# Re-timing the loads of the weights and of pair 2, one copy moved to VectorE and one changed order of masks, in a fused state-space and feed-forward kernel

## The chip, the cores and the metric

The kernel runs on one core of a Trainium2 chip. The metric is the device time in microseconds (us). Five runs of the kernel before gave 131.43, 131.52, 131.6, 133.93 and 136.94 us, with a median of 131.6 us. One execution was profiled.

TensorE appears in the profile as PE (matrix multiplications) and PEld (its weight loads), VectorE as DVE, ScalarE as ACT, GpSimd as POOL and the sync engine as SP. A small q behind a name means the engine's instruction sequencer, which also issues DMAs.

## The reference

The first half is a state-space layer over `x` (4 batches, 8 heads, 768 rows, 32 columns), with a decay `a` for each row and with `B` and `C` of 16 columns for each head. The second half is a bilinear feed-forward layer: 3072 tokens of 256 columns, a hidden width of 1536.

```python
for c in range(nc):                                  # chunks of 32 rows
    cum = np.cumsum(la, axis=-1)                     # la = log(a) of the chunk
    L = np.exp(cum[..., :, None] - cum[..., None, :]) * causal
    CB = np.einsum('bhin,bhjn->bhij', Cc, Bc)
    y_intra = np.einsum('bhij,bhjd->bhid', CB * L, xc)
    y_inter = np.einsum('bhin,bhnd->bhid', Cc, state) * np.exp(cum)[..., None]
    y[:, :, sl] = y_intra + y_inter
    state = decay_full * state + sum_j(B_j x_j decay_from_j)
...
x = y.transpose(0, 2, 1, 3).reshape(B * S, H * D)
out = ((x @ w_a) * (x @ w_b)) @ w_out
```

Inputs and output are float32.

## The kernel before

**Tiling.** The kernel works in 6 blocks of 128 rows and not in chunks of 32. A "pair" is one block of two batches, so there are 12 pairs, numbered 0 to 11: pairs 0 and 1 are block 0, pairs 2 and 3 are block 1, and so on. A tile of a pair holds 64 partitions for each of its two batches (`bt` 0 and 1); every partition holds two neighbouring rows.

**A pair's way through the engines.**

1. Loads (`load1`, line 119): six DMAs for a pair, B, C and x, one for each batch. B and C are 64 KB each and x is 128 KB each in the profile's counting. B and C arrive in pieces of 128 bytes, x in pieces of 256 bytes. The input tiles `bn`, `cn` and `xn` have three buffers each.
2. Scaling: `scale_bc` (line 236) makes `cm` and `bm` in f16 from C and B and the decay factors `fC` and `fB`; `scale_x` (line 227) makes `x16`. From pair 1 on, GpSimd scales B and C.
3. `transposes` (line 253): TensorE transposes `bm` (two instructions) and `cm` (two) into PSUM. ScalarE copies the transposed B out twice (`bt`, line 265), then the transposed C is copied out (`ct`, line 266). For pair 0 the transposes go to two PSUM banks and VectorE copies C. For all other pairs they go to one bank, `TT`, which is a part of the tile `SC0`, and ScalarE copies C.
4. `scores` (line 271): 32 small matmuls into the four banks `SC[0]` to `SC[3]`. Two tiles hold them: `SC0` has banks 0 and 1, `SC1` has banks 2 and 3.
5. `mask` (line 304): four products with the causal mask, 128x512 each, on VectorE. In pairs 0 to 2 one of the four goes another way (`by_pool`): ScalarE copies the scores to `tmp`, and GpSimd multiplies.
6. `pv` (line 348): matmuls with the carried state (`sbd`, line 355), with `x16` (line 321) and for the next state (line 338), all into `SC1`; ScalarE copies the result into `X2T`.
7. `state` (line 381): VectorE updates `U32`; GpSimd spreads it into `sbd` for the pair two further on.
8. `unit(p, k2)` (line 410), six for each pair: eight matmuls make 256 of the 1536 hidden columns for Wa and Wb, ScalarE copies the one half (`asb`), and the product with the other half is a VectorE instruction. `unit` returns this product as a function, so that the caller chooses where in VectorE's queue it goes: `h = unit(...)` and later `h()`. `go` calls both at once.
9. `out_half` (line 456): twelve matmuls with Wo, a copy on ScalarE and a store from SP's queue.

**What sets the order.** The order is written out by hand, and each engine executes its own instructions in this order. Semaphores stand between engines where one reads what another wrote. Two instructions of different engines that touch the same PSUM tile are kept apart too, also where both only read. PSUM holds `SC0`, `SC1` and four more banks, taken in turn by the tag `ff`.

**The start.** The weights are split in thirds of 512 hidden columns. The units 0 and 1 of a pair use the first third of Wa and Wb, units 2 and 3 the second, units 4 and 5 the third. GpSimd's queue issues the weights (`load_w`, line 169), with a conversion to f16 in the DMA. Two dependencies are written by hand: the second Wa waits for one of pair 0's x loads (line 182), and pair 3's first load waits for Wo (line 504). SP's queue issues most of the input loads, ScalarE's queue a few of pair 0 and 1. Matmuls on a tile of zeros (`warmup`, line 184) fill TensorE's first microseconds.

Of the kernel before, what the change touches and what calls it, by code (L numbers as in the profile page):

```python
# [15 lines left out]
AFTER = mybir.DependencyInfo(mybir.DependencyClass.Sync, mybir.DependencyReason.DATA)  # L16
# [6 lines left out]
def kernel(  # L23
# [13 lines left out]
    nc = tc.nc  # L37
# [4 lines left out]
    NBLK = S // Q  # L42
# [36 lines left out]
    Wa = big.tile([128, 2, d_ff], f16, name="Wa")  # L79
    Wb = big.tile([128, 2, d_ff], f16, name="Wb")  # L80
    Wo = big.tile([128, NK, d_model], f16, name="Wo")
# [9 lines left out]
    fC = big.tile([128, NBLK, 2, NBP, H], f32, name="fC")  # L91
# [21 lines left out]
    def tiles(p):  # L113
        Bn = inp.tile([128, H, 2, N], f32, name="bn", tag="bn")
        Cn = inp.tile([128, H, 2, N], f32, name="cn", tag="cn")
        Xn = inp.tile([128, H, 2, D], f32, name="xn", tag="xn")
        pair_in[p] = (Bn, Cn, Xn)

    def load1(eng, p, which, bt):
        blk, bp = divmod(p, NBP)  # L120
        src = (B, C, x)[which][2 * bp + bt, :, blk * Q : (blk + 1) * Q, :]
        return eng.dma_start(  # L122
            pair_in[p][which][64 * bt : 64 * bt + 64].rearrange("i h r n -> i h (r n)"),
            src.rearrange("h (i r) n -> i h (r n)", r=2),
        )

    def load(p, eng=None):
        tiles(p)
        return [load1(eng or nc.sync, p, w, bt) for w in range(3) for bt in range(2)]
# [6 lines left out]
    load1(nc.scalar, 0, 1, 1)  # L136
    load1(nc.sync, 0, 1, 0)
    nc.scalar.preload_act_table_set("natural_log_exp_and_others")
    x_in = load1(nc.scalar, 0, 2, 1)
    nc.scalar.dma_start(c32, p32_t.ap())  # L140
    load1(nc.sync, 0, 2, 0)
    load1(nc.scalar, 1, 1, 1)
# [2 lines left out]
    load1(nc.sync, 1, 0, 1)  # L145
    load1(nc.sync, 1, 2, 0)
    load1(nc.sync, 1, 2, 1)
    load(2)
    nc.vector.memset(warm.bitcast(u32), 0)  # L149
    nc.vector.memset(zero, 0.0)  # L150
    nc.gpsimd.memset(sel, 1.0)
# [14 lines left out]
    KC = 4 * 128  # L166
    wd = []

    def load_w(q3):
        for W, src in ((Wa, moe_w_a), (Wb, moe_w_b)):  # L170
            c = slice(q3 * KC, (q3 + 1) * KC)
            wd.append(nc.gpsimd.dma_start(W[:, :, c], src.rearrange("(f p) e -> p f e", p=128)[:, :, c]))

    load_w(0)
    nc.gpsimd.memset(causal, 1.0)
    for bt in range(2):
        v = causal[64 * bt : 64 * bt + 64]
        nc.gpsimd.affine_select(
            out=v, in_=v, compare_op=ALU.is_ge, fill=0.0, base=0, pattern=[[-1, 2], [1, Q]], channel_multiplier=-2
        )  # L180
    load_w(1)
    tc.add_manual_dep(wd[2].ins, x_in.ins.name, AFTER, reason="inputs first")

    def warmup(n, bank, cols=512):
        for _ in range(n):
# [5 lines left out]
    def scan(lo, hi):  # L191
        for k in range(lo, hi):
            nc.vector.tensor_tensor_scan(Pr[:, k], a_sb[:, k], zero, 1.0, ALU.mult, ALU.add)
# [27 lines left out]
    def flat(f, lo, hi):  # L221
        return f[:, lo:hi].rearrange("p k r b h -> p (k r b h)")
# [4 lines left out]
    def scale_x(p, eng):  # L227
        X16 = mid.tile([128, H, 2, D], f16, name="x16", tag="x16")
        xo, xi = X16.rearrange("p h r d -> p (h r d)"), pair_in[p][2].rearrange("p h r d -> p (h r d)")
        st.setdefault(p, {})["X16"] = X16  # L230
        if eng is nc.scalar:
            nc.scalar.mul(xo, xi, XS)  # L232
        else:
            eng.tensor_scalar(xo, xi, XS, None, ALU.mult)  # L234

    def scale_bc(p, which, eng):
        blk, bp = divmod(p, NBP)
        name, f = (("bm", fB), ("cm", fC))[which]
        m_ = mid.tile([128, 2, H, N], f16, name=name, tag=name)
        eng.tensor_tensor(  # L240
            out=m_,
            in0=pair_in[p][which].rearrange("p h r n -> p r h n"),
            in1=f[:, blk, :, bp].unsqueeze(3).broadcast_to((128, 2, H, N)),
            op=ALU.mult,
        )
        st.setdefault(p, {})[name] = m_

    def scale(p):
        scale_bc(p, 1, nc.gpsimd)
        scale_bc(p, 0, nc.gpsimd)  # L250
        scale_x(p, nc.gpsimd)

    def transposes(p, ps=None):
        s = st[p]
        TB, TC = (TT[:, 0:256], TT[:, 256:512]) if ps is None else [t_.bitcast(f16)[:, 0:256] for t_ in ps]
        for T_, src in ((TB, s["bm"]), (TC, s["cm"])):
            for r in range(2):
                nc.tensor.transpose(  # L258
                    T_[:, r * 128 : (r + 1) * 128], src[:, r].rearrange("p h n -> p (h n)"), ident
                )  # L260
        BT = mid.tile([128, 2, 2, 2, 64], f16, name="bt", tag="bt")
        CT = mid.tile([128, 2, Q], f16, name="ct", tag="ct")
        for e in range(2):
            o_ = BT[:, e].rearrange("p r t i -> p (r t i)")
            nc.scalar.activation(out=o_, in_=TB, func=AF.Copy, scale=par[:, e : e + 1])  # L265
        (nc.scalar.copy if ps is None else nc.vector.tensor_copy)(  # L266
            CT.rearrange("p t (i r) -> p r (t i)", r=2), TC.rearrange("p (r c) -> p r c", r=2)
        )
        s["BT"], s["CT"] = BT, CT
# [20 lines left out]
    def product(p, m):  # L290

        return (
            st[p]["T1"][:, 2 * m : 2 * m + 2].rearrange("p e r q -> p e (r q)"),
            SC[m].rearrange("p (e c) -> p e c", e=2),
        )

    def product0(m2, e):

        return (
            st[0]["T1"][:, 4 * m2 : 4 * m2 + 4].rearrange("p (m e) r q -> p e m (r q)", e=2)[:, e],  # L300
            (SC0, SC1)[m2][:, :, e * 256 : e * 256 + 256],
        )

    def mask(out_in, by_pool=False):
        o_, i_ = out_in
        c_ = causal.rearrange("p r q -> p (r q)").unsqueeze(1).broadcast_to((128, 2, 2 * Q))
        if by_pool:
            tmp = mid.tile([128, 2, 2 * Q], f32, name="tmp", tag="tmp")
            nc.scalar.copy(tmp, i_)  # L309
            nc.gpsimd.tensor_tensor(out=o_, in0=tmp, in1=c_, op=ALU.mult)  # L310
        else:
            nc.vector.tensor_tensor(out=o_, in0=i_, in1=c_, op=ALU.mult)  # L312
# [97 lines left out]
    def unit(p, k2):  # L410
        s = st[p]
        if k2 == 0:
            s["hk"] = ffh.tile([128, NK, 2 * Q], f16, name="hk", tag="hk")
        a_ps = psf.tile([128, 512], f32, name="aps", tag="ff")
        b_ps = psf.tile([128, 512], f32, name="bps", tag="ff")
        for ps, W in ((a_ps, Wa), (b_ps, Wb)):
            for kk in range(2):
                k = 2 * k2 + kk
                for f in range(2):
                    nc.tensor.matmul(  # L420
                        ps[:, kk * 2 * Q : (kk + 1) * 2 * Q],
                        W[:, f, k * 128 : (k + 1) * 128],
                        X2T[:, p, f].rearrange("p t q -> p (t q)"),
                        start=(f == 0),
                        stop=(f == 1),
                        skip_group_check=True,
                    )
        asb = ffh.tile([128, 512], f32, name="asb", tag="asb")
        nc.scalar.copy(asb, a_ps)  # L429
        return lambda: nc.vector.tensor_tensor(  # L430
            out=s["hk"][:, 2 * k2 : 2 * k2 + 2, :].rearrange("p k q -> p (k q)"), in0=b_ps, in1=asb, op=ALU.mult
        )
# [23 lines left out]
    def out_half(p, bt):  # L456
        o_ps = psf.tile([128, 512], f32, name="ops", tag="ff")
        out_mm(p, bt, o_ps, range(NK))
        out_store(p, bt, o_ps)


    def bank(name):
        return psf.tile([128, 512], f32, name=name, tag="ff")
# [16 lines left out]
    v = factors_mm(0, 1)  # L480
# [5 lines left out]
    scale_bc(0, 1, nc.vector)  # L486
    scan(1, 2)
    tb, tcp = bank("tb"), bank("tc")
    transposes(0, [tb, tcp])
    scan(2, 3)  # L490
    warmup(1, SC[3])
    scores(0)
# [2 lines left out]
    mask(product0(0, 0))  # L495
    mask(product0(0, 1))
    mask(product0(1, 0))
    load_w(2)
    scale_bc(1, 1, nc.gpsimd)
    scale_bc(1, 0, nc.gpsimd)  # L500
    wo_d = nc.gpsimd.dma_start(Wo, moe_w_out.rearrange("(k p) e -> p k e", p=128))
    nc.gpsimd.tensor_copy(maskbd, headm.unsqueeze(2).broadcast_to((128, H, D)))
    n0 = load(3)
    tc.add_manual_dep(n0[0].ins, wo_d.ins.name, AFTER, reason="weights first")
    warmup(3, tcp)
    py = [bank("py0"), bank("py1")]
    pv_u(0, 0, py, True)
# [4 lines left out]
    for bt in range(2):  # L512
# [4 lines left out]
    h = unit(0, 0)  # L517
# [1 line left out]
    h()  # L519
    go((0, 1))  # L520
    v = factors_mm(1, NBLK)
    nc.scalar.copy(flat(fC, 1, NBLK), v)
    transposes(1)
    nc.vector.tensor_tensor(out=hr, in0=Pr[:, 0:NG, Q - 1], in1=rmid[:, 0:NG], op=ALU.mult)
    nc.vector.tensor_tensor(out=hs, in0=hr, in1=Pr[:, 1:NBLK, 63], op=ALU.mult)
    nc.vector.tensor_tensor(
# [2 lines left out]
        in1=selb.rearrange("p (b g) -> p b g", b=nb),  # L529
        op=ALU.mult,  # L530
    )
    h = unit(0, 2)
    fb(1)
    scores(1)
# [3 lines left out]
    h = unit(0, 3)  # L538
# [19 lines left out]
    h = unit(1, 4)  # L558
    scores(2)
    mask(product(2, 3), by_pool=True)  # L560
    h()
    scale_x(2, nc.scalar)
    mask(product(2, 0))
    h = unit(1, 5)
    mask(product(2, 1))
    mask(product(2, 2))
    h()
    out_half(0, 0)
    scale(3)
    pull(2)  # L570
    pv(2)
# [9 lines left out]
    h = unit(2, 2)  # L581
# [5 lines left out]
    h = unit(2, 3)  # L587
# [9 lines left out]
    for p in range(4, NP):  # L597
# [5 lines left out]
        h = unit(p - 1, 0)  # L603
# [4 lines left out]
        h = unit(p - 1, 1)  # L608
# [56 lines left out]
```

## Time and profile before

| | |
|---|---|
| median of five runs | 131.6 us |
| the profiled execution, its own time | 131.6 us |
| its span, first to last instruction | 129.9 us |
| what lies around the span | 1.7 us |
| mean granted TensorE clock | 0.994 of full speed |
| PE busy | 121.5 us (94% of the span) |
| DVE, ACT, POOL busy | 86.5, 74.6, 53.3 us |
| moved by DMA | 12.22 MB |

The profile's page gives the busy time of every engine, the span in 40 slices (each digit is a busy share in tenths), the DMA queues, the chain of work that ended last, and groups of instructions. The trace behind it answers closer questions: the instructions in order of time, with the idle time ahead of each and what ended it; the waits summed by who waited for whom; the DMAs with the time from issue to landing. "L240" is line 240 of the kernel. Times are from the start of the span.

A DMA's life has three moments: the engine issues it, its packets pass through the 16 DMA engines, and it lands, which is when the waiting instruction may go on. Queue q0 is that of GpSimd's DMAs, q1 that of SP's and q10 that of ScalarE's.

### The profile page before, as it was taken

How to read it: one execution, taken by the hardware profiler on the slowest of the kernel's cores; microseconds unless marked ns; L12 is line 12 of the kernel's file. 1: busy time of each engine (PE TensorE's matmuls, PEld its weight loads, DVE VectorE, ACT ScalarE, POOL GpSimd, SP SyncE). 2: the span in 40 equal slices, each digit the busy share in tenths (PEclk: the TensorE clock that was granted, in tenths of full speed). 3: DMA queues.
4: the chain of work that ended last, by engine and by line, in shares of the span. 5: the costliest groups of instructions: out<-in, count | busy, mean ns of one | idle time of the engine just before them, and what ended most of it. 6: DMA issues, size and time to landing. Idle time of an engine off the chain costs nothing.

```text
span 129.9 us, 4718 instructions
## 1 busy us (share of the span) xinstructions
PE 121.5 (94%) x1947; PEld 100.8 (78%) x1947; DVE 86.5 (67%) x163; ACT 74.6 (57%) x154; POOL 53.3 (41%) x72
## 2 busy tenths in 40 slices
PE   6769898989999999999999999999999999999980
PEld 2326767878888888888888988898888888888870
DVE  1487669693774975956957938948939829744440
ACT  3344585874648476476476576475486485464520
POOL 7769433948755709219129039047056000000000
PEclk9999999999999999999999999999999999999997
DMA  3999999264746542613613614515510110110102
GB/s 67 172 201 204 212 209 183 37 131 94 160 78 175 101 112 64 130 54 74 124 52 85 116 51 94 108 45 110 132 42 9 45 40 5 40 40 7 59 20 81
DMA packets 44805, 12.22 MB, mean 94 GB/s; under 512 B 38576, under 2 KB 44752, under 8 KB 44784
## 3 DMA queue, kind: packets, MB, share of 16 engines
q1 hardware_dynamic: 39264, 9.08, 33.4%
q0 software_dynamic: 3216, 2.36, 12.1%
q10 hardware_dynamic: 2304, 0.48, 1.8%
q8 instruction: 15, 0.25, 0.9%
q14 instruction: 6, 0.05, 0.1%
HBM read 11.13 MB, written 3.15 MB: 110 GB/s over the span
## 4 chain that ended last, share of the span: by engine, by line
PE 85%; DVE 4%; DMA 3%; ACT 2%; issue 1%; SPq 1%; DVEq 0%
PE aps L420 24%; PE ops L437 23%; PE bps L420 23%; PE SC L279 4%; DMA cn<-in_C_dram 3%; PE SC L321 3%; PE SC L258 3%; DVE t L312 2%; PE SC L355 2%; PE SC L338 1%; PE fps L210 1%; DVE hk L430 1%; PE py L321 1%; SPq L122 1%; ACT x L232 0%
## 5 line engine op out<-in xcount | busy, mean ns | idle before, releaser
L430 DVE TENSOR_TENSOR hk<-bps,asb 128x512 f16<-128x512 f32 x72 | 49.0, 687 | 24.2 <-ACT asb L429 22.2
L429 ACT COPY asb<-aps 128x512 f32<-128x512 f32 x72 | 41.9, 588 | 17.2 <-PE aps L420 15.6
L420 PE MATMUL aps<-X2T,Wa 128*128 128x256 f16 x288 | 43.5, 273 | 0.0
L420 PE MATMUL bps<-X2T,Wb 128*128 128x256 f16 x288 | 43.2, 272 | 0.0
L437 PE MATMUL ops<-Wo,hk 128*128 128x256 f16 x288 | 35.2, 273 | 0.0
L312 DVE TENSOR_TENSOR t<-SC,causal 128x512 f16<-128x512 f32 x45 | 29.4, 681 | 2.3 <-ACT tmp L309 2.0
L420 PEld LDWEIGHTS <-Wb 128*128 128x128 f16 x288 | 28.1, 98 | 3.6 <-issue 0.2
L437 PEld LDWEIGHTS <-hk 128*128 128x128 f16 x288 | 27.7, 98 | 3.2
L420 PEld LDWEIGHTS <-Wa 128*128 128x128 f16 x288 | 26.9, 98 | 4.3 <-DVE X2T L379 0.3
L395 POOL TENSOR_TENSOR sbd<-U,maskbd 128x512 f16<-128x512 f32 x10 | 11.6, 1159 | 32.3 <-DVE U L391 32.2
L452 ACT ACTIVATE osb<-ops 128x256 f32<-128x256 f32 x23 | 8.8, 383 | 18.4 <-PE ops L437 18.4
L234 POOL TENSOR_SCALAR x<-xn 128x512 f16<-128x512 f32 x9 | 13.4, 1490 | 2.1 <-DMA xn<-in_x_dram 1.5
L367 ACT ACTIVATE X2T<-SC 128x512 f16<-128x512 f32 x11 | 6.6, 597 | 7.5 <-PE SC L338 6.5
L265 ACT ACTIVATE bt<-SC,ch 128x256 f16<-128x256 f16 x22 | 9.2, 471 | 0.1
L240 POOL TENSOR_TENSOR cm<-cn,fC 128x256 f16<-128x256 f32 x11 | 6.9, 625 | 4.4 <-DMA cn<-in_C_dram 4.4
L391 DVE SCALAR_TENSOR_TENSOR U<-SC,G,gU 128x64 f32<-128x64 f32 x16 | 3.8, 280 | 6.2 <-ACT X2T L367 6.2
L240 POOL TENSOR_TENSOR bm<-bn,fB 128x256 f16<-128x256 f32 x11 | 6.9, 628 | 0.0
L279 PEld LDWEIGHTS <-bt 32*64 32x64 f16 x384 | 3.4, 104 | 3.2 <-issue 2.8
L321 PEld LDWEIGHTS <-x 64*32 64x32 f16 x384 | 3.4, 91 | 3.2 <-ACT x L232 1.0
L279 PE MATMUL SC<-ct,bt 32*64 32x128 f16 x384 | 5.1, 220 | 0.7 <-ACT ct L266 0.4
L310 POOL TENSOR_TENSOR t<-tmp,causal 128x512 f16<-128x512 f32 x3 | 3.5, 1151 | 5.2 <-ACT tmp L309 5.2
L186 PE MATMUL SC<-warm 128*128 128x512 f16 (+1 forms) x11 | 4.3, 538 | 1.2 <-DVE warm L149 1.2
(59 smaller groups left out, 70.5 us busy)
## 6 DMA issues: line engine op xcount, KB each, us to landing
xn<-in_x_dram SPq DMA_DIRECT2D x23, 128.0 KB, 3.6
out_dram<-osb SPq DMA_DIRECT2D x23, 128.0 KB, 1.7
bn<-in_B_dram SPq DMA_DIRECT2D x23, 64.0 KB, 2.8
cn<-in_C_dram SPq DMA_DIRECT2D x22, 64.0 KB, 2.9
Wa<-in_moe_w_a_dram POOLq DMA_DIRECT2D x3, 256.0 KB, 6.0
Wb<-in_moe_w_b_dram POOLq DMA_DIRECT2D x3, 256.0 KB, 6.9
Wo<-in_moe_w_out_dram POOLq DMA_DIRECT2D x1, 768.0 KB, 10.6
cn<-in_C_dram ACTq DMA_DIRECT2D x2, 64.0 KB, 5.5
```

The source lines that it names most:

```text
L234: eng.tensor_scalar(xo, xi, XS, None, ALU.mult)
L240: eng.tensor_tensor(out=m_, in0=pair_in[p][which].rearrange("p h r n -> p r h n"), in1=f[:, blk, :, bp].unsqueeze(3).broadcast_to((128, 2, ...
L265: nc.scalar.activation(out=o_, in_=TB, func=AF.Copy, scale=par[:, e : e + 1])
L279: nc.tensor.matmul(SC[m][64 * bt : 64 * bt + 64, c0 : c0 + Q], BT[rows, e, r, bt], CT[rows, bt], start=True, stop=True, skip_group_check=True,
L312: nc.vector.tensor_tensor(out=o_, in0=i_, in1=c_, op=ALU.mult)
L321: nc.tensor.matmul(py[bt][32 * g : 32 * g + 32, u * Q : (u + 1) * Q], s["X16"][k, h, r, :], s["T1"][k, h, r, :], start=(first and u == 0 a ...
L395: nc.gpsimd.tensor_tensor(out=Sbd.rearrange("p t (m c) -> p t m c", m=4), in0=U32[:, p].unsqueeze(2).broadcast_to((128, 2, 4, 2 * D)), in1 ...
L420: nc.tensor.matmul(ps[:, kk * 2 * Q : (kk + 1) * 2 * Q], W[:, f, k * 128 : (k + 1) * 128], X2T[:, p, f].rearrange("p t q -> p (t q)"), sta ...
L429: nc.scalar.copy(asb, a_ps)
L430: return lambda: nc.vector.tensor_tensor(out=s["hk"][:, 2 * k2 : 2 * k2 + 2, :].rearrange("p k q -> p (k q)"), in0=b_ps, in1=asb, op=ALU.mult)
L437: nc.tensor.matmul(o_ps[:, 0:d_model], hk[:, k, bt * Q : (bt + 1) * Q], Wo[:, k, :], start=(k == 0), stop=(k == NK - 1), skip_group_check= ...
L452: nc.scalar.activation(out=o_sb, in_=o_ps[:, 0:d_model], func=AF.Copy, scale=1.0 / (YS * YS))
```

## The change

The change has six edits.

1. Pair 2's six loads leave the start of SP's queue (line 148) and are issued where pair 3's loads were (line 503), with pair 3's behind them.
2. The first of pair 2's loads waits for the third Wa (`wd[4]`). The dependency of pair 3's first load on Wo is gone.
3. GpSimd issues the weights in another order among its other steps: first Wa, then the causal mask, then first Wb and second Wa. The second Wb goes behind GpSimd's product of pair 0, directly ahead of the third Wa and third Wb. The second Wa no longer waits for pair 0's x.
4. In `transposes(1)` VectorE copies `ct`, not ScalarE.
5. `transposes(1)` is called behind the small VectorE steps `hr`, `hs` and `hsx`, and ScalarE's copy of the factors `fC` of blocks 1 to 5 behind `transposes(1)`.
6. In pair 2, the three VectorE masks go ahead of the products of `unit(1, 4)` and `unit(1, 5)`.

```diff
-    x_in = load1(nc.scalar, 0, 2, 1)
+    load1(nc.scalar, 0, 2, 1)
...
-    load(2)
...
-    def load_w(q3):
-        for W, src in ((Wa, moe_w_a), (Wb, moe_w_b)):
+    def load_w(q3, which=(0, 1)):
+        for W, src in [((Wa, moe_w_a), (Wb, moe_w_b))[w] for w in which]:
...
-    load_w(0)
+    load_w(0, (0,))
     nc.gpsimd.memset(causal, 1.0)
...
-    load_w(1)
-    tc.add_manual_dep(wd[2].ins, x_in.ins.name, AFTER, reason="inputs first")
+    load_w(0, (1,))
+    load_w(1, (0,))
...
-    def transposes(p, ps=None):
+    def transposes(p, ps=None, ct_eng=None):
...
-        (nc.scalar.copy if ps is None else nc.vector.tensor_copy)(
+        (ct_eng or nc.scalar.copy)(
...
-    transposes(0, [tb, tcp])
+    transposes(0, [tb, tcp], nc.vector.tensor_copy)
...
     mask(product0(1, 0))
+    load_w(1, (1,))
     load_w(2)
     scale_bc(1, 1, nc.gpsimd)
     scale_bc(1, 0, nc.gpsimd)
-    wo_d = nc.gpsimd.dma_start(Wo, moe_w_out.rearrange("(k p) e -> p k e", p=128))
+    nc.gpsimd.dma_start(Wo, moe_w_out.rearrange("(k p) e -> p k e", p=128))
     nc.gpsimd.tensor_copy(maskbd, headm.unsqueeze(2).broadcast_to((128, H, D)))
-    n0 = load(3)
-    tc.add_manual_dep(n0[0].ins, wo_d.ins.name, AFTER, reason="weights first")
+    n0 = load(2)
+    tc.add_manual_dep(n0[0].ins, wd[4].ins.name, AFTER, reason="weights first")
+    load(3)
...
     v = factors_mm(1, NBLK)
-    nc.scalar.copy(flat(fC, 1, NBLK), v)
-    transposes(1)
     nc.vector.tensor_tensor(out=hr, ...)
     nc.vector.tensor_tensor(out=hs, ...)
     nc.vector.tensor_tensor(out=hsx, ...)
+    transposes(1, None, nc.vector.tensor_copy)
+    nc.scalar.copy(flat(fC, 1, NBLK), v)
     h = unit(0, 2)
...
     h = unit(1, 4)
     scores(2)
     mask(product(2, 3), by_pool=True)
-    h()
+    mask(product(2, 0))
     scale_x(2, nc.scalar)
-    mask(product(2, 0))
-    h = unit(1, 5)
+    h2 = unit(1, 5)
     mask(product(2, 1))
     mask(product(2, 2))
     h()
     out_half(0, 0)
+    h2()
     scale(3)
```

## The prediction

> **What bounds the kernel now.** I read the page first, then TensorE's waits, then the order of time from 0 to 30 us, then the DMAs by issue and by queue.
>
> The page (TensorE's share, then the busy tenths of PE and of the DMA engines in 40 slices of 3.25 us):
>
> ```profile
> span 129.9 us, 4718 instructions
> PE 121.5 (94%) x1947; PEld 100.8 (78%) x1947; DVE 86.5 (67%) x163; ACT 74.6 (57%) x154; POOL 53.3 (41%) x72
> PE   6769898989999999999999999999999999999980
> DMA  3999999264746542613613614515510110110102
> ```
>
> TensorE is full from the tenth slice on, and DMA is dense only in the first seven. After 30 us no wait of TensorE is long enough to be listed. So the change acts only through TensorE's idle time before 30 us, and what TensorE loses there it can't make up later.
>
> The waits from 16 to 30 us (who waited for whom: us in total, times, longest):
>
> ```profile
> POOL cm L240 <- DMA cn<-in_C_dram: 3.5, 2, 3.0
> DVE t L312 <- ACT tmp L309: 2.0, 1, 2.0
> PE SC L355 <- DVE t L312: 0.4, 1, 0.4
> PE SC L279 <- ACT ct L266: 0.4, 1, 0.4
> ```
>
> TensorE's own losses are three of about 0.4 us: pair 1's scores wait for `ct`, pair 1's `pv` for a mask (19.6 us), pair 2's `pv` for a mask. No weight and no load costs TensorE anything measurable now. The first line matters most: GpSimd already waits 3.0 us for C of pair 2.
>
> The order of time (start, duration, engine, line; idle time ahead in brackets):
>
> ```profile
> 10.11 0.76 POOL L172 DMA_DIRECT2D Wa<-in_moe_w_a_dram  x1
> 15.05 0.84 ACT L265 ACTIVATE bt<-SC,ch 128x256 f16<-128x256 f16 x2
> 15.78 0.44 ACT L266 COPY ct<-SC 128x256 f16<-128x256 f16 x1
> 16.27 0.43 PE L279 MATMUL SC<-ct,bt 32*64 32x128 f16 x32 [0.39 <-ACT ct L266]
> ...
> 21.66 0.62 POOL L240 TENSOR_TENSOR cm<-cn,fC 128x256 f16<-128x256 f32 x1 [3.04 <-DMA cn<-in_C_dram]
> 22.24 0.62 POOL L240 TENSOR_TENSOR bm<-bn,fB 128x256 f16<-128x256 f32 x1
> 23.94 0.28 PE L258 MATMUL SC<-ident,bm 128*128 128x128 f16 x2
> ...
> 26.01 1.29 DVE L430 TENSOR_TENSOR hk<-bps,asb 128x512 f16<-128x512 f32 x2 [1.00 <-ACT asb L429]
> 27.22 1.88 DVE L312 TENSOR_TENSOR t<-SC,causal 128x512 f16<-128x512 f32 x3
> 29.15 0.38 PE L355 MATMUL SC<-ct,sbd 128*128 128x128 f16 x4 [0.43 <-DVE t L312]
> ```
>
> Pair 2's path: C landed at 21.53, `cm`, `bm` (done 22.86), TensorE's transposes at 23.85. The slack is 1.0 us.
>
> The DMA queues, first from 18 to 19 us and then from 24.9 to 26.9 us (packets, MB, share):
>
> ```profile
> q0 software_dynamic: 345, 0.18, 127.2%
> q1 hardware_dynamic: 302, 0.04, 48.9%
> ...
> q1 hardware_dynamic: 1402, 0.17, 55.0%
> ```
>
> Beside Wo, q1 gets some 300 packets per us; alone 701.
>
> **The change, part by part.** The sum is made against the profiled execution, 131.6 us (129.9 span plus 1.7 around it), which equals the median of the five runs.
>
> *Masks ahead of products (pair 2).* VectorE's second `hk` of the group at 26.01 (0.64) moves behind the three masks (1.88). They can begin at 26.65, as the scores are done at 26.43; the ScalarE copy that shares `SC1` with the third ends at 27.24. They end at 28.53 in place of 29.10. TensorE's preceding matmuls end at 28.72, so the 0.43 us ahead of L355 goes: **-0.43**. The moved `hk` now ends near 29.1; the next matmuls into its bank came at 29.97 and would come at 29.54. Cover: 0.4 us. `hk` of unit (1,5) keeps its time.
>
> *C of pair 1 on VectorE.* Reads of one PSUM tile by two engines are serialized here: the mask waited 2.0 us for `tmp`, another bank of the same tile. So VectorE's copy can't run beside ScalarE's two `bt`, which end at 15.89. On ScalarE `ct` began at 15.78, overlapping them by 0.11. On VectorE it begins about 0.03 after 15.89 (the handover seen from `tmp`'s end at 17.39 to the mask's start at 17.42) and takes 0.44 as in pair 0 (L266 on DVE). `ct` ends at 16.36, not 16.22: the scores, `tmp`, the masks and the wait at 19.6 all move by **+0.14**. Bounds: -0.39, the whole gap, if the two copies did run side by side; +0.3. ScalarE is freed of 0.44 but idles there: nothing. `fC` moves from 14.72 to about 15.8, hidden by ScalarE's wait for the scores; its readers are `fB` (VectorE, idle until 17.42) and GpSimd past 20 us. The `hr`, `hs`, `hsx` steps end at 14.85, ahead of the copy: nothing.
>
> *GpSimd's queue.* The causal mask (0.34 + 1.12) goes ahead of the first Wb: its issue moves from 3.52 to about 5.04. The quickest weight landing took 5.9 us, so it lands at 10.9; needed at 11.53. The row of 6.8 (which was queued behind Wa) would cost 0.3; I take 0. The second Wa goes out at 5.76 in place of 6.95: hidden, needed at 14.8. The second Wb goes from 7.66 to 10.11: landing between 14.6 (first packet 2.55 after issue as for the first Wa, 256 packets at the 167 per us seen from 6 to 7 us, 0.36 receipt) and 17.0 (6.9). TensorE wants it at 15.18, but waits for `ct` until 16.4 right after those 0.44 us of matmuls, so up to 15.95 is free: 0, at most +1.0. `cm` and `bm` of pair 1 come one issue (0.72) later, done at 13.7, needed at 14.61: hidden by TensorE's factors, with 0.9 left.
>
> *The first microseconds.* C of pair 0 landed at 6.29 and sets the start. All issues up to 3.5 us are unchanged, and by 6.29 only packets of the first Wa had passed on q0: 0, with bounds of 0.2 either way.
>
> *Pair 2's loads.* The third Wa is issued one issue later, at 10.87. By packets, second Wb and third Wa end at 12.66 + 512/167 = 15.7 and land at 16.1; by the 6.9 us of its own row before, at 17.8. I take 16.5: q0 is emptier than it was, though a 16 KB instruction fetch held one DMA engine for 1.36 us from 13.7 on. SP's queue stands until then; behind the waiting load are the other five of pair 2, pair 3's six and the first store. Pair 3's first issue followed Wo's landing by 0.07 and its first packet by another 1.4, so pair 2's packets start at 18.0. B and C are 2048 packets. The third Wb ends by 17.7 and Wo's 1536 packets, at 345 per us, by 22.1. Until then q1 passes 4.1 x 300 = 1230; the other 818 take 1.2 us at 701. Last packet 23.3, landing 23.6 with the receipt. `cm` and `bm` end 1.33 later as before (21.53 to 22.86): 24.95. TensorE wants them at 23.85 + 0.14 = 24.0: **+0.95**. Ends: 0, if Wo didn't hold q1 back (pair 3's C landed 5.2 after its first issue: 16.1 + 5.3 = 21.4); +2.25 at 17.8. The stall delays TensorE, ScalarE and VectorE together, so the masks' gain stays. x of pair 2 and all of pair 3 follow by about 27 us; GpSimd took pair 3's C at 28.96: hidden.
>
> The Trainium skill, "DMA: Bandwidth & Descriptors", section "Anatomy of one DMA — SWDGE (gpsimd) path", gives a fixed 2.0 us plus the bytes over 436 GB/s, which is an estimate of 2.6 us for a third of Wa. By that the third Wa would be in at 13.5, pair 2's C at 18.8, and the sum would be 131.3. The rows of 5.9 to 7.5 us in this trace disagree, since these transfers queue, and I go by the rows.
>
> Sum: 131.6 - 0.43 + 0.14 + 0.95 = 132.26, so **132.3 us**.
>
> **Rivals.**
>
> A. *Pair 2 arrives in time, the kernel is faster.* If C has landed by 22.65, no stall: 131.6 - 0.43 + 0.14 = 131.3. For it: 13 to 18 us is nearly free for weights, and TensorE's slack is 1 us. Against: half of pair 2's B and C pass beside Wo at 300 per us. It decides from a landing at 22.95 on, where stall and gain cancel.
>
> B. *The stall just pays for the masks.* Landing from 22.7 to 23.2, as with a third Wa at 15.7 to 16.1: 131.35 to 131.85.
>
> C. *The lagging DMA engine makes it worse.* Third Wa at 17.8, C at 24.9, stall 2.2: 133.5. For it: the third Wa took 6.9 us before. Against: q1 was busy beside it then.
>
> D. *The second Wb stops TensorE.* Landing at 16.5 to 17.0 adds 0.5 to 1.0 at unit (0,2): with the main case 132.8 to 133.3; but TensorE would then also want pair 2 that much later, so most of it overlaps with the stall.
>
> **How the numbers follow.** About 0.2% (0.26 us) is what a measurement of this kernel tells from no change. Main case (stall 0.6 to 1.7, 131.9 to 133.0): 0.55. A: 0.15. B: 0.17. C: 0.10. D: 0.03. Slower is main, C and D, 0.68; same is B; faster is A. The range goes from A's 131.2 to 133.4, which leaves out a part of C and little below.
>
> **What would show it.** Right: GpSimd's `cm` of pair 2 at 23 to 24 us, and TensorE's L258 near 25 with an idle gap ahead of it, named after `bm`; no gap ahead of L355; L279 of pair 1 at 16.4 waiting for VectorE's `ct`. Wrong: q1 passing well over 300 packets per us beside Wo; a third Wa landed before 16; a gap ahead of the matmuls with the first or second Wb.

## The result, and the profile after

The change makes the kernel slower: the ratio of its time to the time before is 1.0084, with a 95% interval of 1.0063 to 1.0104. On 131.6 us this is +1.1 us (+0.8 to +1.4). The medians over all runs are 133.26 us (43 runs) and 132.4 us (80 runs of the kernel before); the ratio, unlike these medians, leaves out the executions in the slower state that both kernels show at times. The forecast was slower, by 0.66 us: the direction was right, the size too small.

The profiled execution has a span of 132.3 us, 2.4 more than before. Its own time, 133.98 us, lies above the median: it also lost some 0.7 us at the start, of which the last section tells. The page, with the lines that answer those of before:

```profile
span 132.3 us, 4719 instructions
PE 122.4 (93%) x1947; PEld 101.0 (76%) x1947; DVE 86.9 (66%) x164; ACT 74.3 (56%) x153; POOL 52.8 (40%) x72
PE   6949988489999999999999999999999999999990
PEclk9995999999999999999999999999999999999999
DMA  3999999562556554541542442613611010110102
```

Slices are 3.3 us long. PE has a hole in the eighth (23.1 to 26.5 us) that it did not have, and one in the third, at the start. DMA stood at 2 in the eighth slice before and stands at 5 now: the loads of pair 2 are still under way there.

TensorE's waits from 9 to 32 us:

```profile
PE SC L257 <- POOL bm L239: 2.0, 1, 2.0
PE py L320 <- ACT x L231: 1.4, 1, 1.4
PE SC L278 <- DVE ct L265: 0.5, 1, 0.5
PE SC L320 <- DVE t L311: 0.4, 1, 0.4
```

(Most line numbers are one less than before, as a line is gone from the start.) The wait ahead of the matmuls with `sbd` is gone. The wait for `ct` grew from 0.39 to 0.54 us. The new one is 2.04 us ahead of pair 2's transposes, for GpSimd's `bm`. In the order of time:

```profile
17.43 1.33 SPq L122 DMA_DIRECT2D bn<-in_B_dram  x2
18.80 1.67 SPq L122 DMA_DIRECT2D cn<-in_C_dram  x2
25.58 0.62 POOL L239 TENSOR_TENSOR cm<-cn,fC 128x256 f16<-128x256 f32 x1 [6.26 <-DMA cn<-in_C_dram]
26.15 0.62 POOL L239 TENSOR_TENSOR bm<-bn,fB 128x256 f16<-128x256 f32 x1
26.83 0.28 PE L257 MATMUL SC<-ident,bm 128*128 128x128 f16 x2 [2.04 <-POOL bm L239]
```

The third Wa landed at 17.41, SP issued pair 2's first load at 17.43, and C landed at 25.44. GpSimd stood 6.26 us. The DMA queues show where the time went. First from 18 to 19 us, then from 21 to 22 us:

```profile
q0 software_dynamic: 331, 0.17, 135.1%
...
q1 hardware_dynamic: 972, 0.12, 78.8%
q0 software_dynamic: 139, 0.07, 51.4%
```

From 18 to 19 us, over half a microsecond after the issue, q1 has no line at all: not one packet of pair 2 moved. By the trace's packet records the first one moved at 20.32, when 395 of Wo's 1536 packets were still to come.

### The profile page after: what moved, and what is told of

Read it like the earlier page. It is cut to its first block, busy times and chain, and to the rows that moved or that the text cites. A ratio compares the mean times of both kernels' runs of the same rounds, so it can differ in the third digit from the quotient of the medians.

```text
span 132.3 us, 4719 instructions
## 1 busy us (share of the span) xinstructions
PE 122.4 (93%) x1947; PEld 101.0 (76%) x1947; DVE 86.9 (66%) x164; ACT 74.3 (56%) x153; POOL 52.8 (40%) x72
## 4 chain that ended last, share of the span: by engine, by line
PE 74%; DMA 13%; DVE 2%; SPq 2%; POOL 2%; ACT 2%; issue 2%; POOLq 0%; DVEq 0%
PE ops L436 24%; PE aps L419 20%; PE bps L419 20%; DMA cn<-in_C_dram 7%; DMA Wa<-in_moe_w_a_dram 6%; PE SC L278 3%; PE SC L320 3%; PE SC L257 2%; SPq L122 2%; PE SC L354 2%; PE SC L337 1%; DVE hk L429 1%; POOL t L309 1%; POOL Wb L171 1%; DVE t L311 1%
## 5 line engine op out<-in xcount | busy, mean ns | idle before, releaser
L451 ACT ACTIVATE osb<-ops 128x256 f32<-128x256 f32 x23 | 8.8, 383 | 18.5 <-PE ops L436 18.5
```

What stands on the lines that cost most here:

```text
L451: nc.scalar.activation(out=o_sb, in_=o_ps[:, 0:d_model], func=AF.Copy, scale=1.0 / (YS * YS))
```

## The experiments

Each kernel ran beside the kernel before on the same chip; ratios are to that kernel. The intervals are some 0.4% to each side in most runs, so where an effect is smaller, the profile decides. Each kernel has one profile, the changed one two.

**The changed kernel again.** No edit.

> The changed kernel once more, unchanged, beside the two others. Expected: ratio 1.006 to 1.011, and in the profile a stall of 1.5 to 3 us ahead of pair 2's transposes, the larger the earlier the first unit starts, since the DMAs don't wait for TensorE; no gap ahead of the matmuls with sbd of pair 2.

Measured: 1.0115 (1.0039 to 1.0191). This profile has a start like that of before (first unit at 10.94 us; before 10.99), so it is the cleaner one for comparison. Its waits of TensorE from 9 to 32 us:

```profile
PE SC L257 <- POOL bm L239: 1.6, 1, 1.6
PE py L320 <- ACT x L231: 0.8, 1, 0.8
PE SC L320 <- DVE t L311: 0.4, 1, 0.4
PE bps L419 <- DMA Wb<-in_moe_w_b_dram: 0.2, 1, 0.2
PE SC L278 <- DVE ct L265: 0.2, 1, 0.2
```

The span is 131.1 us, 1.2 over before, which fits the timed 1.1. The third Wa landed at 16.58, the first packet of pair 2 moved at 20.14, C landed at 24.35. The second Wb stopped TensorE for 0.20 us, but the wait for `ct` right behind it was then only 0.16, so the two make 0.36, beside 0.39 for `ct` alone before. That the stall is larger with an earlier start is not borne out by this pair of profiles (1.65 us here, 2.04 with the later start), as C landed 1.1 us earlier here.

**The masks alone (edit 6 on the kernel before).**

```diff
     mask(product(2, 3), by_pool=True)
-    h()
+    mask(product(2, 0))
     scale_x(2, nc.scalar)
-    mask(product(2, 0))
-    h = unit(1, 5)
+    h2 = unit(1, 5)
     mask(product(2, 1))
     mask(product(2, 2))
     h()
     out_half(0, 0)
+    h2()
```

> The kernel before with edit 6 alone: pair 2's three VectorE masks ahead of the products of units (1,4) and (1,5). My theory: the 0.43 us gap of TensorE ahead of the matmuls with sbd goes and nothing gives it back, so 0.4 us faster, ratio 0.997. Rival: the postponed products make a later matmul wait for its PSUM bank, so the gap only moves: ratio 1.000 and a new gap of about 0.4 us within the next few us.

Measured: 0.998 (0.9939 to 1.0021), so the timing alone can't tell the two apart. In the profile the gap of 0.43 us is gone and no new one follows up to 32 us (by start times the gain is 0.59: from pair 2's transposes to its matmuls with `sbd` it is 4.62 us, before 5.21):

```profile
PE SC L279 <- ACT ct L266: 0.4, 1, 0.4
PE SC L321 <- DVE t L312: 0.4, 1, 0.4
PE py L321 <- ACT x L232: 0.3, 1, 0.3
```

**The copy of C alone (edits 4 and 5 on the kernel before).**

```diff
-    nc.scalar.copy(flat(fC, 1, NBLK), v)
-    transposes(1)
     hr, hs, hsx
+    transposes(1, None, nc.vector.tensor_copy)
+    nc.scalar.copy(flat(fC, 1, NBLK), v)
```

> The kernel before with edits 4 and 5 alone: VectorE copies ct of pair 1, behind hr, hs and hsx, and fC is copied later. My theory: VectorE's copy starts only behind ScalarE's two bt copies, so pair 1's scores come 0.14 us later, the gap ahead of them is 0.53 us and not 0.39: ratio 1.001, within what can be measured. Rival: the copies run side by side, the gap closes: 0.3 to 0.4 us faster, ratio 0.997.

Measured: 0.9986 (0.9944 to 1.0029). The profile answers. First ScalarE, then VectorE, around the copy:

```profile
15.03 0.84 ACT L265 ACTIVATE bt<-SC,ch 128x256 f16<-128x256 f16 x2 [1.76 <-PE SC L258]
...
15.90 0.45 DVE L266 COPY ct<-SC 128x256 f16<-128x256 f16 x1 [1.08 <-ACT bt L265]
```

VectorE's copy begins 0.03 us after ScalarE's second copy ends (15.87), although it reads other columns of the bank. The gap ahead of the scores is 0.53 us in place of 0.39. The rival falls.

**The loads and weights alone (edits 1 to 3 on the kernel before).**

> The kernel before with edits 1 to 3 alone: GpSimd's weights in the new order, pair 2's loads behind the third Wa, pair 3's with no dependency. My theory: this holds the whole loss. C of pair 2 lands at 24 to 25.5 us, TensorE stands 1.5 to 2 us ahead of pair 2's transposes, and the masks' gap of 0.43 us stays: 1.3 to 1.8 us slower, ratio 1.010 to 1.014. Rival (the loss lies in the first 11 us, from the order of the weights): the first unit starts 0.4 us or more later than at 11.0 and at a lower granted clock, and the stall ahead of the transposes is under 1 us.

Measured: 1.0164 (1.0108 to 1.0221); span 132.8 us. The waits of TensorE:

```profile
PE SC L257 <- POOL bm L239: 3.0, 1, 3.0
PE py L320 <- ACT x L231: 1.6, 1, 1.6
PE SC L354 <- DVE t L311: 0.4, 1, 0.4
```

The stall, 2.97 us, is larger than expected, and so is the loss; the masks' gap is there. The first unit started at 10.89 us and at full clock, against the rival. All of the loss is in these three edits. It is some 1 us more than the changed kernel loses. The masks and the copy explain 0.3 to 0.4 us of that; the rest stays open, and this profile's stall was also the longest of the three with these DMA edits (1.65, 2.04 and 2.97).

**Pair 2's loads at the start again (edits 1 and 2 undone).**

```diff
     load1(nc.sync, 1, 2, 1)
+    load(2)
...
-    n0 = load(2)
-    tc.add_manual_dep(n0[0].ins, wd[4].ins.name, AFTER, reason="weights first")
-    load(3)
+    n0 = load(3)
+    tc.add_manual_dep(n0[0].ins, wo_d.ins.name, AFTER, reason="weights first")
```

> The changed kernel with edits 1 and 2 undone: pair 2's loads at the start of SP's queue with no dependency, pair 3's behind Wo as before; the weights' order, the copy and the masks as changed. My theory: no stall ahead of pair 2's transposes, so the masks' 0.43 us less the copy's 0.14 are left: 0.3 us faster than before, ratio 0.998. Rival (the weights' order costs time at the start): 0.3 to 0.8 us slower than before, ratio 1.002 to 1.006, with no stall at the transposes.

Measured: 1.0002 (0.9965 to 1.0039). No stall ahead of the transposes; C of pair 2 landed at 19.53. The loss is gone, with the order of the weights still changed. Whether 0.3 us are gained, or up to 0.5 lost as the rival has it, is not to be seen: the interval is wider, and the profiled execution ran TensorE at half clock from 7.8 to 14.6 us.

**The order of the weights undone (edit 3 undone, the rest as changed).**

> The changed kernel with edit 3 undone: GpSimd issues the weights in the order of before, pair 2's loads still wait for the third Wa. My theory: the third Wa lands at 16.0 to 17.5 as in the changed kernel, C of pair 2 some 8 us later, and TensorE stands 1.5 to 3 us ahead of pair 2's transposes: ratio 1.007 to 1.015. Rival (the weights' order holds a good part of the loss): stall under 1 us and ratio under 1.004.

Measured: 1.0031 (0.9991 to 1.0071), stall 0.79 us: both numbers are the rival's. So the weights' order seems to hold a good part of the loss, though only together with the late loads (with these at the start it cost nothing that could be measured). It rests on one profile, and the interval overlaps that of the changed kernel. The third Wa landed at 15.73, pair 2's loads were issued at 15.75, their first packet moved at 19.69 and C landed at 23.53, 7.8 us after the third Wa, as expected. Beside the cleaner profile of the changed kernel, all of pair 2's path is earlier: the third Wa (15.73; there 16.58), the first packet (19.69; 20.14) and C (23.53; 24.35). Wo was issued 0.7 us earlier (12.81; 13.50), but landed at the same time (22.40; 22.35). Whether the order costs time through the third Wa or through Wo's packets is not shown.

**No dependency for pair 2's loads.**

```diff
     n0 = load(2)
-    tc.add_manual_dep(n0[0].ins, wd[4].ins.name, AFTER, reason="weights first")
     load(3)
```

> The changed kernel without the dependency of pair 2's first load on the third Wa; pair 2's loads keep their place in SP's queue, now directly behind pair 1's, so they go out from about 9 us on. My theory (the stall is made by the late issue): C of pair 2 lands by 21 us, no idle time of TensorE ahead of pair 2's transposes, 1.5 to 2 us faster than the changed kernel, ratio to before 0.996 to 1.000. Rival (the order of the weights alone makes pair 2 late): a stall of 1 us or more stays.

Measured: 0.9963 (0.992 to 1.0007). The loads are issued from 8.27 us on, C lands at 20.91, and no stall is left at the transposes. The second Wb landed at 15.51, much as in the changed kernel (15.25 and 15.45), but TensorE came to it at 14.78 and not at 15.29. So it stopped TensorE for 0.78 us at unit (0,2), which takes the place of the wait for `ct`. So the dependency, not the place of the loads behind pair 1's, makes the loss.

**Pair 2's loads behind the second Wa.**

```diff
-    tc.add_manual_dep(n0[0].ins, wd[4].ins.name, AFTER, reason="weights first")
+    tc.add_manual_dep(n0[0].ins, wd[2].ins.name, AFTER, reason="weights first")
```

> The changed kernel with pair 2's first load behind the second Wa, not the third. The second Wa landed at 12.7. Theory A (a late gate plus Wo's packets): the loads go out from 12.8, ahead of Wo's packets, C lands by 20 us, no stall at pair 2's transposes, the masks' gain is left: ratio 0.996 to 1.000. Theory B (the weights' own packets hold the loads back just as Wo's do): C lands past 22 us, a stall of over 0.5 us stays.

Measured: 0.9958 (0.9909 to 1.0008); no stall at the transposes. C landed at 21.21, later than theory A had it. The loads were issued at 11.75 and the first packet moved at 15.64, with 107 packets of the weights still to come and none of Wo's moved yet. So the weights' packets hold them back too, as theory B said, but not for long enough to matter. The second Wb stops TensorE for 0.41 us here.

**Wo later.**

```diff
     scale_bc(1, 0, nc.gpsimd)
-    nc.gpsimd.dma_start(Wo, ...)
...
     mask(product(1, 3), by_pool=True)
+    nc.gpsimd.dma_start(Wo, ...)
```

> The changed kernel with Wo's DMA issued later, behind GpSimd's product of pair 1 (at about 19.3 us and not at 13.7), so that pair 2's loads meet no Wo packets in their first 3 us. Theory A (Wo's packets hold pair 2's loads back): first packets 1.4 us after the issue, C of pair 2 lands 5 to 6 us after the third Wa and not 8, at about 22.7, the stall at pair 2's transposes falls from 2.0 to under 0.5 us; Wo lands at 26.5 to 28, which can add up to 1 us ahead of the first matmuls with Wo. Theory B (the queue of pair 2's loads is slow by itself): C lands 7 us or more after the third Wa, and the stall stays over 1.2 us.

Measured: no ratio with an interval came of its four executions (131.94, 133.52, 137.01 and 137.1 us), so I read the profile alone. TensorE's two largest waits past 16 us are now for Wo and `ct`, and q1 flows from 19 to 20 us with no packet on q0:

```profile
PE ops L436 <- DMA Wo<-in_moe_w_out_dram: 1.6, 1, 1.6
PE SC L278 <- DVE ct L265: 0.5, 1, 0.5
...
q1 hardware_dynamic: 771, 0.10, 60.8%
```

The first packet of pair 2 moved 1.37 us after the issue (16.74 to 18.11), C landed at 21.16, 4.4 us after the third Wa, and the stall is gone. Theory A holds. Wo itself lands at 29.67, 1.7 us later than the range I gave, and costs 1.65 us: it was issued 6.3 us later than in the kernel before and took as long to land (10.4 us, before 10.6).

**Wo in two halves.**

```diff
-    nc.gpsimd.dma_start(Wo, wo_r)
+    nc.gpsimd.dma_start(Wo[:, 0 : NK // 2], wo_r[:, 0 : NK // 2])
...
     mask(product(1, 3), by_pool=True)
+    nc.gpsimd.dma_start(Wo[:, NK // 2 :], wo_r[:, NK // 2 :])
```

> The changed kernel with Wo's DMA in two halves, the first where it was, the second behind GpSimd's product of pair 1 (about 19.3 us). Theory A (pair 2's first packets wait until the packets queued earlier on GpSimd's queue have drained): half of Wo drains 2.2 us earlier, so the first packets come at 18.3 to 19.3 and not at 20.3, C lands at 22 to 23.5, the stall at pair 2's transposes falls to 0 to 1 us. Theory B (a fixed delay of about 3 us after the issue beside any traffic): first packets 2.9 us or more after the issue, C 7.5 us or more after the third Wa, stall as in the changed kernel.

Measured: 1.0024 (0.9979 to 1.007). Packets of the two queues, from 17.5 to 18.5 us and from 19 to 20 us:

```profile
q0 software_dynamic: 362, 0.19, 141.7%
...
q1 hardware_dynamic: 1349, 0.17, 108.7%
q0 software_dynamic: 29, 0.01, 9.7%
```

The loads were issued at 16.26, q1 has no packet up to 18.5, the first one moves at 18.71, and once the half of Wo is all but through, 1349 pass in one microsecond. C lands at 21.36 and the stall is zero. (The interval of the time still touches that of the changed kernel, so the profile decides.) The second half of Wo lands at 26.43 and nobody waits for it. The fixed delay of theory B falls: issues between 15.75 and 17.43 beside a whole Wo got their first packet between 19.69 and 20.32 (four profiles). The issue alone does not set the moment; in these runs the packets ahead did.

**The order of pair 1 and 2, no DMA changed.**

```diff
+    transposes(1)
     v = factors_mm(1, NBLK)
     nc.scalar.copy(flat(fC, 1, NBLK), v)
-    transposes(1)
...
     mask(product(1, 2))
-    h()
-    h = unit(0, 3)
+    h2 = unit(0, 3)
     mask(product(1, 0))
...
     mask(product(1, 1))
     h()
+    h2()
```

(and edit 6)

> The kernel before with edit 6 and two more changes of order, no change to any DMA: pair 1's transposes go ahead of the 40 small factor matmuls, and pair 1's VectorE masks go ahead of the products of units (0,2) and (0,3). My theory (only TensorE's three gaps before 30 us were to be had): the gaps of 0.39 ahead of pair 1's scores, 0.42 ahead of pair 1's pv and 0.43 ahead of pair 2's matmuls with sbd all close, 1.2 us faster than before, ratio 0.991. Rival (the postponed products and the delayed factors take it back): new gaps of 0.3 us or more between 17 and 31 us, ratio 0.996 or more.

Measured: 0.9979 (0.9936 to 1.0022), short of my theory. The number is the rival's, but not its cause. The three gaps are closed, and the profile has another in their place, for a load:

```profile
PE SC L258 <- POOL bm L240: 1.2, 1, 1.2
PE py L321 <- ACT x L232: 0.4, 1, 0.4
```

TensorE comes to pair 2's transposes earlier, and in this execution C of pair 2 landed at 23.81 (21.53 in the profile of before, 22.55 with the masks alone, 21.37 with the copy alone, all with the same DMAs). From 18 to 19 us q1 passed only 37 packets beside 375 of q0; in the profile of before it was 302 beside 345. So the loads of pair 2 are the next limit already in the kernel before.

**Both together: a version that beats both kernels.** The order of the last one, the weights in the order of before, pair 2's loads behind the second Wa, Wo in two halves.

```diff
-    load(2)
...
+    nc.gpsimd.dma_start(Wo[:, 0 : NK // 2], wo_r[:, 0 : NK // 2])
     nc.gpsimd.tensor_copy(maskbd, ...)
+    n0 = load(2)
+    tc.add_manual_dep(n0[0].ins, wd[2].ins.name, AFTER, reason="weights first")
+    load(3)
...
     mask(product(1, 3), by_pool=True)
+    nc.gpsimd.dma_start(Wo[:, NK // 2 :], wo_r[:, NK // 2 :])
```

> The order of e9_best (edit 6, pair 1's transposes ahead of the factor matmuls, pair 1's masks ahead of its products) with the weights in the order of before, pair 2's loads behind the second Wa, pair 3's directly behind them, and Wo in two halves as in e10_wo_halves. My theory (pair 2's loads are late only through the packets that GpSimd's queue holds ahead of them): C of pair 2 lands by 21 us, no stall at pair 2's transposes, the three gaps stay closed, 1.2 us faster than before, ratio 0.988 to 0.993. Rival (with three gaps gone TensorE comes too early for some load or weight in any order): a stall of 0.5 us or more ahead of pair 2's transposes or of a matmul with a weight, ratio 0.995 or more.

Measured: 0.9855 (0.9788 to 0.9921), median 130.38 us. All that TensorE still waits for from 9 to 32 us:

```profile
PE py L320 <- ACT x L231: 0.5, 1, 0.5
PE bps L419 <- DMA Wb<-in_moe_w_b_dram: 0.2, 1, 0.2
```

C lands at 21.76, later than my theory had it, but in time. The interval is a gain of 1.0 to 2.8 us. The best estimate is 1.9; the idle time of the three gaps before makes 1.18 of it. From the first unit to the last matmul this profile took 113.93 us, that of before 115.28, although TensorE ran at half clock up to 12.65 us here. How much of the 1.9 is real can't be told closer.

## Why the prediction was right or wrong, point by point

**The bound.** Right. TensorE's idle time before 30 us is where the whole difference lies; where the idle time ahead of pair 2's transposes went, the slowdown went too, except with Wo later, which traded it for a wait for Wo.

**Masks ahead of products, -0.43.** The gap went, in the profile of the masks alone and in both of the changed kernel. Its size was put too low: by start times it is worth 0.58 to 0.59 (see the sum).

**C of pair 1 on VectorE, +0.14.** Right: 0.53 in place of 0.39. It was read from two waits of the trace before in which the copies of one tile were serialized. In the cleaner profile of the changed kernel it is not to be seen: TensorE waited 0.20 us for the second Wb and then only 0.16 for `ct`.

**GpSimd's queue, 0.** Near. The first Wb landed at 10.75 and 10.64 (forecast 10.9), the second at 15.25 and 15.45 (14.6 to 17.0), with a stall of at most 0.20 us, hidden by the wait for `ct` behind it. The edit also moves Wo's issue back, from 12.93 to 13.5 and 13.7; Wo's last packet passed at 21.96 in the cleaner profile (forecast 22.1) and at 23.33 in the other. Undoing the order took the stall to 0.79 us, so the order may not be free once the loads are late; through which step is not shown.

**Pair 2's loads, +0.95.** The mis-sized term. In the changed kernel with the same start as before it measured 1.65, in the profiled one 2.04, in the three DMA edits alone 2.97. The steps of it, with the values of the cleaner profile: the third Wa landed at 16.58 (forecast 16.5; 17.41 in the profiled execution), which was right. The step that failed is "its first packet by another 1.4, so pair 2's packets start at 18.0": they started at 20.14. I took the 1.4 us from pair 3's loads before the change, which were issued when GpSimd's queue was empty (they waited for Wo). Beside a queue filled with Wo it is 2.9 to 4.0 us. The step behind it failed the other way: "Until then q1 passes 4.1 x 300 = 1230" was read from packets that had been queued ahead of Wo. In the changed kernel q1 passed none, and then 972 in a microsecond (983 in the cleaner profile), so the last of B and C was through at 23.7 and not 23.3, and C landed at 24.35 and not 23.6.

The bounds of that term (0 to 2.25) held the two executions of the changed kernel. Rival C had the size. Its cause, a late third Wa, is not in the cleaner profile (16.58). In the first one it is in part (17.41), but the first packet moved only 0.18 us later there. Of the signs named, the gap ahead of L258 for `bm` and the missing gap ahead of L355 came as forecast. GpSimd's `cm` came later than 23 to 24 us (24.49 and 25.58), and q1 did pass well over 300 packets in a microsecond beside the end of Wo, which had been named as a sign of being wrong.

**The estimate of 2.6 us for a third of Wa.** This estimate from the Trainium skill would have had no stall. The thirds of the weights took 4.9 to 8.5 us in these runs, so the rows were the better guide. The Trainium skill, "DMA: Bandwidth & Descriptors", section "Queues, rings and completion order", says that each DMA engine takes turns between the queues it has work for. Where both queues had been filled for long, the packets from 18 to 19 us agree in the kernel before (345 and 302), but not with the order of pair 1 and 2 alone changed (375 and 37). For a queue that starts while the other is full, they do not agree either: 331 and 0 in the changed kernel, then 139 and 972. The measurement decides here.

**The sum.** -0.43 + 0.14 + 1.65 gives 1.36, and with a start 0.05 us earlier 1.31; the last matmul of the cleaner profile ended 1.21 us later than before, and the timed ratio says 1.1. Start times close the difference. An idle time is counted from the modelled end of the matmul ahead, but a matmul that need not wait starts before that end (pair 2's transposes before the change: 23.94, with the end at 24.10). So the stall and the masks' gap each cost 0.15 to 0.16 us more than their idle time. Pair 2's transposes started at 25.74 and not at 23.94, 1.80 later; from there to the matmuls with `sbd` it is 4.63 us and not 5.21. That makes 1.80 - 0.58 = 1.22.

## What to carry to other kernels

In this kernel a latency from issue to first packet held only for the queue state in which it was measured: look whether another queue was full then and whether it will be full after the change. A load that must be in time is issued ahead of a large transfer on another queue, or the large transfer is cut in two. And when a gap ahead of one consumer closes, all later consumers come earlier: check the slack of the next load before counting the gain.

## What the runs showed of the hardware

**A queue that starts behind a full one can wait long.** With the whole Wo queued ahead, pair 2's loads issued at 15.75, 16.24, 16.60 and 17.43 us got their first packets at 19.69, 20.23, 20.14 and 20.32, when 252, 347, 320 and 395 of Wo's 1536 packets were still to come. With half of Wo ahead, 16.26 became 18.71; with no Wo ahead, 16.74 became 18.11. This is no rule without exception: in the combined version the loads were issued at 13.19, behind the first half of Wo, and their first packet moved at 15.99, with 707 of that half's 768 packets still to come. Loads queued before Wo shared with it evenly in one profile and hardly at all in another (302 beside 345, and 37 beside 375). Which part of the DMA hardware does this was not tried, and stays open.

**TensorE's start at half clock.** The granted clock moves in stretches of 3.41 us whose phase differs from execution to execution. In the profiled execution of the changed kernel it fell back to half from 9.28 to 12.70 us. In the stretch before, TensorE had been idle for 1.65 of the 3.41 us, the most of it from 8.16 us on, in its wait for pair 0's x. The windows show the fall (columns: window, its length, busy us of PE, PEld, DVE, ACT and POOL, granted clock, DMA share, GB/s):

```profile
9.00:10.00 1.00, 0.48 (x17) 0.26 (x17) 0.43 (x1) 0.47 (x2) 1.00 (x2) 0.64 1.35 212
10.00:11.00 1.00, 1.00 (x18) 0.37 (x18) 0.00 (x0) 0.48 (x3) 1.00 (x3) 0.50 1.38 219
11.00:12.00 1.00, 1.00 (x6) 0.58 (x5) 0.93 (x4) 0.24 (x1) 0.57 (x1) 0.50 1.35 234
```

In the profile of before the same three windows read 1.00. A matmul of the first units took 421 ns there and 274 ns before, the first unit began at 11.35 and not 10.99, and by pair 2's transposes some 0.7 us were lost. It is no effect of the change alone: the masks alone, with the DMAs of before, also had matmuls of 421 ns until 13 us (its clock is on record from 13.55 us on only), and the three DMA edits, with an idle time of 1.6 us at 7.9, did not. The Trainium skill, "TensorE: Matmul & The Clock Gate", section "Part 1: The HAM clock gate", describes such a gate with a free-running window of about 3.4 us, which fits the 3.41 us here. Over the fourteen profiles the first unit began between 10.09 and 11.51 us. This spread at the start is larger than most parts of the change, which is why the small ones were read from waits and not from times.
